# Forming more q-k blocks from stored q and k, and halving value products by an adding DMA

## The chip, the core and the metric

The kernel runs on one core of a Trainium2 chip. A core has a matmul engine (PE), a vector engine (DVE), a scalar engine (ACT), a general engine that here only issues DMAs (POOL), and SP, which issues DMAs too. Each engine works through its own queue in order and waits on semaphores for the others. Matmuls write to PSUM, eight banks of 128 x 512 fp32; everything else lies in SBUF, 128 partitions wide. The metric is device microseconds of one execution.

## The reference

One input `x` (2048 tokens, 1024 wide) goes through two branches that a sigmoid gate mixes. Branch A is dilated local attention with 32 heads of 32: each position looks at itself and at seven earlier positions in steps of two. Branch B is a gated GELU network with 3584 hidden columns.

```python
g = _sigmoid((x * gate_w).sum(-1, keepdims=True))
a = _A_ref(x, wqkv, wo)      # H = 32, Dh = 32, W = 8, dil = 2
b = _B_ref(x, w_gate, w_up, w_down)
return g * a + (1 - g) * b

# in _A_ref
idx = pos[:, None] - off[None, :]            # off = arange(8) * 2
logits = einsum("bhsd,bhswd->bhsw", q, kg) * scale
logits = where(mask, logits, -1e9)
o = einsum("bhsw,bhswd->bhsd", softmax(logits), vg)
return o.reshape(B, S, D) @ wo
# in _B_ref
h = gelu(x @ w_gate) * (x @ w_up)
return h @ w_down
```

## The kernel before, in words

All large products are done by Strassen's scheme (seven products for eight). The work before the last part is a row of 78 units. A unit forms two output tiles of 128 x 1024 from seven half-depth products, each of four matmuls of 128 x 512 (L366), 28 matmuls in all; ACT copies or evaluates the PSUM results (L374, L384, L389, L396, L372) and one DVE addition (L403) closes the unit. It reads the banks that the unit's last products wrote, and the unit's L22 product (in `p4`) writes one of these banks again, 12 matmuls after the last product that L403 waits for.

Units 0 and 1 belong to branch B (gate and up). Units 2 to 17 make q and k: two halves of the sequence (s = 0, 1), eight tiles (t) of 128 dimensions each. Units 18 to 25 make v, and the others up to 77 gate and up. Then `run_last` joins attention and hidden values in the down projection, again by Strassen's scheme, in two levels (L1046, L1079 and the DVE forms L1004 and L1012).

Between the units' L403s DVE does the attention. The planner is `run_bg`: after each unit it takes steps of background tasks in order of priority until a credit of about 4.7 us, by the costs that the tasks yield, is used up. `due` forces a task to end at a given unit. What the planner takes in a unit stands in DVE's queue between that unit's L403 and the next, so the order is fixed when the program is built.

The sequence is cut into eight blocks of 256 positions (`AC`), four for each half.

- q-k products, `qk_prods` and `qk_mult` (L598). For three of the four blocks of a half, each unit's q and k tile gives a product tile of 128 x 2048 (eight window positions by 256). `reduce_mm` (L603) sums the 32 dimensions of each head on PE, by matmuls with a block pattern that write 32 rows each, four beside each other, and accumulates over the eight tiles t in PSUM. For each pair of units 24 such matmuls stand in one slot of PE's queue.
- The fourth block of each half is formed later. `store_qk` writes its q and k columns to DRAM, `spill_load` brings them back, and `spill` multiplies them and adds four tiles together (L649) before the reduction, so that its two accumulated tiles need only 8 matmuls.
- `softmax` and `softmax_back` (L687 to L709) make the weights and store them (`w_d`, by POOL). They run in five groups: two blocks, one block, three blocks, one, one.
- Value products, `pv_all`. `pv_load` (SP) brings weights and values of a block. For each of eight tiles one product of 2048 elements (L745), and for each two tiles three foldings that halve 8 window positions to 4, 2 and 1 (L752). Products of the next tiles stand between the foldings, so that an operation seldom needs the one just before it. Results are stored to `o_d` by POOL.
- `t_forms` (L874) makes sums of the down weights and stores them to `t_d`; `sums_pair` (L323) makes sums of the gate and up weights; `h_store` (L254) multiplies gate and up.
- `gate_chunk` (L282, in two slots) forms the sigmoid's argument in bank 1, just after the reductions of that slot.

A slot is a place in a unit after its fifth product, where reductions queued in `slotq` and the gate's matmuls go:

```python
cur.p5()
extra = 0.0
if slotq:
    slotq.pop(0)()
    extra += 1.6 if b <= QE + 3 else 0.8
...
cur.p26()
...
run_bg(b, (4.7 if b < NQKV else 4.8) + extra)
```

Of the kernel before, what the change touches and what calls it, by code (L numbers as in the profile page):

```python
# [32 lines left out]
R_Q = 32  # L33
# [3 lines left out]
R_EX = (194.5, 81, 50, 81, 84)  # L37
# [15 lines left out]
R_O = (36, 32)  # L53
R_VB = (40, 48.25)
R_AB = (44.25, 52.5)
R_PROD2 = 56.5
# [12 lines left out]
def kernel(  # L69
# [51 lines left out]
    q_d = [tc.dram_tile([P, NT, AC], BF16, name=f"q_d{s}") for s in range(2)]  # L121
    k_d = [tc.dram_tile([P, NT, KV], BF16, name=f"k_d{s}") for s in range(2)]
# [9 lines left out]
    w_d = tc.dram_tile([NBLK, 32, NJ, SC], BF16, name="w_d")  # L132
# [4 lines left out]
    with tc.manual_schedule(engines={mybir.EngineType.PE, mybir.EngineType.DVE, mybir.EngineType.Activation,  # L137
# [357 lines left out]
        def h_task(G, U, i, s):  # L495
            h_store(G, U, i, s)
            yield 1.14 if i < NE_ else 2.35
# [28 lines left out]
        def store_qk(T, t, s):  # L526
            if s == 0:
                nc.scalar.copy(out=ktail[:, t, :], in_=T[:, 1, SUP - HALO:SUP])
            nc.gpsimd.dma_start(out=q_d[s][:, t, :], in_=T[:, 0, SUP - AC:SUP])
            nc.gpsimd.dma_start(out=k_d[s][:, t, :], in_=T[:, 1, SUP - KV:SUP])  # L530
# [42 lines left out]

        qb = [reg3(R_Q + 9 * i, NT, AC) for i in range(2)]
        kb = [reg3(R_Q + 9 * i + 4, NT, KV) for i in range(2)]
        vb = [reg3(R_VB[i], NT, KV) for i in range(2)]
        pr_off = [R_PR + 4 * i for i in range(4)] + [R_PROD + 4 * i for i in range(2)]
        prod = [reg3(o, NWIN, AC) for o in pr_off]
        attn_all = reg3(R_ATTN, NBLK, SC)
        mask = reg3(R_MASK, NWIN, SJ)  # L580
        ab_ = [reg4(R_AB[i], NJ, NWIN, SJ) for i in range(2)]
        ob_ = [reg3(R_O[i], NT, AC) for i in range(2)]
        prod2 = [reg4(R_PROD2 + 8 * i, 2, NJ, NWIN * SJ) for i in range(2)]
# [6 lines left out]
        pr_n = [0]  # L590

        def prod_tile():
            k = pr_n[0] % 6
            pr_n[0] += 1
            return prod[k]

        def qk_mult(dst, q, k):
            TT(out=dst, in0=q.rearrange("p (o s) -> p o s", o=1).to_broadcast([P, NWIN, AC]),  # L598
               in1=_win_ap(k, [[-DIL, NWIN], [1, AC]]), op=ALU.mult)

# [5 lines left out]
        ND = BPS - 1  # L606
        LGB = 5
        reduced, front, prods = [0], set(), {}

        def qk_prods(u, s, t):  # L610
            while reduced[0] < NT * s + t - t % 2:
                yield None
            out_ = []
            for a in range(ND):
                pr = prod_tile()
                qk_mult(pr, u.T[:, 0, a * AC:(a + 1) * AC], u.T[:, 1, a * AC:(a + 1) * AC])
                out_.append(pr)
                yield 1.14
            prods[t] = out_
            if t % 2:  # L620
                slotq.append(lambda: (qk_reduce(s, t - 1, prods[t - 1]), qk_reduce(s, t, out_)))

        def qk_reduce(s, t, out_):
            assert s == 0 or t > 0 or front == {0, 2}
            for a, pr in enumerate(out_):
                reduce_mm(bank(LGB + a), pr, t == 0, t == NT - 1)
            reduced[0] += 1
            if t == NT - 1:
                if s == 0:
                    bg(softmax(0, 2, LGB, 0), 1, now[0])  # L630
                    bg(softmax(2, 1, LGB + 2, 1), 1, now[0])
                else:
                    bg(softmax(BPS, 3, LGB, 2), 1, now[0])

        def spill_load(s):
            nc.sync.dma_start(out=qb[s], in_=q_d[s][:])
            nc.sync.dma_start(out=kb[s], in_=k_d[s][:])

        def spill(s):
            while reduced[0] < 2 * NT:  # L640
                yield None
            accs = []
            temps = [prod_tile() for _ in range(2)]

            def mult(t, dst):
                qk_mult(dst, qb[s][:, t, :], kb[s][:, t, HALO:HALO + AC])

            def add(g, t):
                TT(out=accs[g], in0=accs[g], in1=temps[t % 2], op=ALU.add)  # L649

            for g in range(NT // QG):
                accs.append(prod_tile())
                mult(QG * g, accs[g])
                yield 1.14
                for t in range(1, QG):
                    mult(QG * g + t, temps[t % 2])
                    yield 1.14
                    if t > 1:
                        add(g, t - 1)
                        yield 1.14  # L660
                add(g, QG - 1)
                yield 1.2
            slotq.append(lambda: spill_reduce(s, accs))
# [3 lines left out]
        def spill_reduce(s, accs):  # L667
            for g, acc in enumerate(accs):
                reduce_mm(bank(LGB + s), acc, g == 0, g == len(accs) - 1)
            bg(softmax(s * BPS + BPS - 1, 1, LGB + s, 3 + s), 1, now[0])  # L670
# [4 lines left out]
        def softmax(a, cnt, b0, e):  # L675
# [9 lines left out]
            m = md[:, (0, 2, 0, 3, 0)[e]:(0, 2, 0, 3, 0)[e] + cnt, :]  # L685
            assert e < 2 or ready >= {2: {0, 1, 2}, 3: {0, 1, 2}, 4: {4, 5, 6}}[e]
# [13 lines left out]
        def softmax_back(a, cnt, ee, e4, sw, m, bc):  # L700
            while a // BPS not in gated:
                yield None
            d = m
            V.tensor_reduce(out=d, in_=sw, axis=AX.X, op=ALU.add)
            yield 0.9 * cnt + 0.05
            V.reciprocal(out=d, in_=d)
            TT(out=d, in0=d, in1=gblk[:, a:a + cnt, :], op=ALU.mult)
            yield 0.65 * cnt
            TT(out=attn_all[:, a:a + cnt, :].rearrange("p a (w s) -> p a w s", w=NWIN), in0=e4, in1=bc(d), op=ALU.mult)  # L709
            yield 0.55 * cnt + 0.05  # L710
            for j in range(NJ):
# [3 lines left out]
            if a == 2 * BPS - 1:  # L715
                two[0] = True

        def pv_load(a, i):
            src = w_d[a].rearrange("h j n -> h (j n)")
            nc.sync.dma_start(out=ab_[i % 2].rearrange("p j w s -> p (j w s)"),  # L720
# [4 lines left out]
        PVO = (0, 1, 2, 4, 5, 6, 3, 7)  # L725

        def pv_all():
            for k in (0, 1):
                while PVO[k] not in ready:
                    yield None  # L730
            pv_load(PVO[0], 0)
            yield None
            for i, a in enumerate(PVO):
# [4 lines left out]
                if i == 0:  # L738
                    pv_task[0].prio = 5
                    tasks.sort(key=lambda t_: t_.prio)  # L740
                    yield None
                v, ab, o_ = vb[i % 2], ab_[i % 2], ob_[i % 2]

                def mult(t):
                    TT(out=prod2[(t // 2) % 2][:, t % 2], in0=ab,  # L745
                       in1=_win_ap(v[:, t, HALO:HALO + AC], [[SJ, NJ], [-DIL, NWIN], [1, SJ]]), op=ALU.mult)

                def fold(t, w):
                    pr = prod2[(t // 2) % 2]
                    h = lambda k: pr[:, :, :, k * w * SJ:(k + 1) * w * SJ]  # L750
                    out_ = h(0) if w > 1 else o_[:, t:t + 2, :].rearrange("p t (j s) -> p t j s", j=NJ)
                    TT(out=out_, in0=h(0), in1=h(1), op=ALU.add)  # L752

                mult(0)
                yield 1.14
                mult(1)
                yield 1.14
                for t in range(0, NT, 2):
                    if i + 1 == NBLK and t == 2:
                        load_A(Bs(0)["A12"], 0, 1, 0, 0, KX, False)  # L760
                    nxt = t + 2 < NT
                    if nxt:
                        mult(t + 2)
                        yield 1.14
                    fold(t, 4)
                    yield 1.14
                    if nxt:
                        mult(t + 3)
                        yield 1.14
                    fold(t, 2)  # L770
                    yield 0.68
                    fold(t, 1)
                    yield 0.4
                a0 = a % BPS % 2 * AC
                nc.gpsimd.dma_start(out=o_d[a // BPS][a % BPS // 2][:, :, a0:a0 + AC], in_=o_)
# [31 lines left out]
        bg(spill(0), 4, QE + 2)  # L807
        bg(spill(1), 4, QE + 2)
# [39 lines left out]
        N1 = 5  # L848
# [15 lines left out]
        def t_forms():  # L864
            for q in range(NQ):
                tf_q[0] = q
                if q in (N1 + 1, N1 + 2):
                    tft.prio = 3.9 if q == N1 + 1 else 4.5
# [17 lines left out]
        def tf_close():  # L886
            while tf_q[0] < N1:
                tft.step()
            tft.prio = 4.5
# [3 lines left out]
        at_end(TFE - 1, tf_close)  # L893
# [355 lines left out]
        for b in range(n):  # L1249
# [10 lines left out]
            if slotq:  # L1260
                slotq.pop(0)()
                extra += 1.6 if b <= QE + 3 else 0.8
# [45 lines left out]
```

## Time and profile before

| | before |
|---|---|
| median of 3 runs | 720.93 us (719.81 to 720.95) |
| profiled execution | 720.06 us, span 718.3 us |
| PE, DVE busy | 707.2 us, 673.2 us |
| ACT, POOL busy | 328.7 us, 134.5 us |
| granted TensorE clock | 1.00 |
| DMA | 162.04 MB, mean 226 GB/s |

Busy time is the union of an engine's instructions as the profiler recorded them. A group's row gives the source line, engine, operation, what it writes and reads with shapes, the count, the busy time and the mean of one, and then the idle time just before its instructions with what ended it. A timeline row gives start, length and engine of one instruction or of several alike in a row. A DMA row gives the size of one issue and the median time from issue to landing.

### The profile page before, as it was taken

To read this page: it belongs to the slowest core of one execution; us is meant where nothing else is said; L and a number is where in the kernel's file an instruction comes from. 1 tells how busy PE (TensorE), PEld (TensorE's weight loads), DVE (VectorE), ACT (ScalarE), POOL (GpSimd) and SP (SyncE) were. 2 spreads that over 40 slices of the span, in tenths; PEclk is the share of its full clock that TensorE was granted. 3 is DMA by queue.
4 is the path that set the end of the run, shared out by engine and by line. 5 is a ranking of instruction groups with operands and counts; after the bars stand their busy time and mean duration, and the time that the engine had idled before them with its cause. 6 is when DMAs were issued, how large, how long until landed. Compare 5 with 4: busy or idle time off the path is not lost. (4 is left out here: it accounts for less than half of the span.)

```text
span 718.3 us, 10752 instructions
## 1 busy us (share of the span) xinstructions
PE 707.2 (98%) x4051; PEld 408.2 (57%) x4107; DVE 673.2 (94%) x722; ACT 328.7 (46%) x600; POOL 134.5 (19%) x233
## 2 busy tenths in 40 slices
PE   8999999999999999999999999999999999999998
PEld 4466656655544444444444444444447886758887
DVE  2789989999999999999999999999999999899997
ACT  4554546444456665555555555555322321131431
POOL 1323544133210332121300000000210002110011
PEclk9999999999999999999999999999999999999999
DMA  9976643378264758574934836371891899995951
GB/s 276 284 183 219 229 142 122 106 247 304 102 205 127 231 197 252 175 221 149 294 115 152 280 123 214 124 288 59 300 427 52 307 401 396 420 429 223 379 213 60
DMA packets 92276, 162.04 MB, mean 226 GB/s; under 512 B 19280, under 2 KB 68848, under 8 KB 87872
## 3 DMA queue, kind: packets, MB, share of 16 engines
q1 hardware_dynamic: 75520, 105.46, 42.7%
q0 software_dynamic: 15984, 48.29, 19.3%
q10 hardware_dynamic: 720, 7.60, 2.7%
q8 instruction: 32, 0.52, 0.3%
q14 instruction: 20, 0.16, 0.1%
HBM read 112.17 MB, written 54.14 MB: 232 GB/s over the span
## 5 line engine op out<-in xcount | busy, mean ns | idle before, releaser
L366 PE MATMUL banks<-arena 128*128 128x512 bf16 x2136 | 472.1, 379 | 4.2 <-DVE arena L403 0.7
L366 PEld LDWEIGHTS <-arena 128*128 128x128 bf16 x2184 | 240.5, 111 | 235.3 <-issue 7.0
L1046 PE MATMUL banks<-arena 128*128 128x256 bf16 x1260 | 138.9, 273 | 0.8 <-DVE arena L1012 0.6
L1046 PEld LDWEIGHTS <-arena 128*128 128x128 bf16 x1260 | 123.1, 98 | 16.7 <-issue 1.5
L389 ACT COPY arena<-banks 128x512 f32<-128x512 f32 x78 | 45.8, 587 | 130.7 <-PE banks L366 130.7
L403 DVE TENSOR_TENSOR arena<-banks,arena 128x1024 bf16<-128x1024 f32 x78 | 95.2, 1221 | 11.0 <-PE banks L366 5.5
L374 ACT CAST arena<-banks 128x512 bf16<-128x512 f32 x102 | 59.7, 586 | 42.4 <-PE banks L366 42.4
L745 DVE TENSOR_TENSOR arena<-arena 128x2048 bf16<-128x2048 bf16 x64 | 77.0, 1220 | 0.5
L752 DVE TENSOR_TENSOR arena<-arena 128x2048 bf16<-128x2048 bf16 (+2 forms) x96 | 73.9, 776 | 1.0
L598 DVE TENSOR_TENSOR arena<-arena 128x2048 bf16<-128x2048 bf16 x64 | 74.7, 1219 | 0.1
L260 POOL DMA_DIRECT2D h_d<-arena x28 | 20.4, 730 | 226.5 <-DVE arena L254 195.4
L1079 PE MATMUL banks<-arena 128*128 128x512 bf16 x282 | 62.5, 379 | 0.3
L396 ACT COPY banks<-banks 128x512 f32<-128x512 f32 x78 | 44.5, 570 | 21.8 <-PE banks L366 20.0
L1004 DVE TENSOR_TENSOR arena<-arena 128x2304 bf16<-128x2304 bf16 x40 | 53.3, 1352 | 0.5
L384 ACT COPY banks<-banks 128x512 f32<-128x512 f32 x78 | 45.0, 576 | 13.6 <-PE banks L366 12.1
L1051 ACT COPY banks<-banks 128x256 f32<-128x256 f32 x60 | 21.4, 356 | 60.9 <-PE banks L1046 60.7
L1079 PEld LDWEIGHTS <-arena 128*128 128x128 bf16 x288 | 28.2, 98 | 33.5
L927 DVE TENSOR_TENSOR arena<-arena 128x2048 bf16<-128x2048 bf16 (+1 forms) x40 | 41.8, 1111 | 1.3 <-DMA arena<-h_d 1.3
L372 ACT ACTIVATE arena<-banks 128x512 bf16<-128x512 f32 x54 | 32.2, 597 | 15.4 <-PE banks L366 15.3
L323 DVE TENSOR_TENSOR arena<-arena 128x1024 bf16<-128x1024 bf16 x60 | 38.6, 685 | 0.5
L1012 DVE TENSOR_TENSOR arena<-arena 128x2304 bf16<-128x2304 bf16 x28 | 37.7, 1351 | 0.2
L254 DVE TENSOR_TENSOR arena<-arena 128x2048 bf16<-128x2048 bf16 x28 | 34.0, 1216 | 1.9 <-ACT arena L251 1.4
(93 smaller groups left out, 435.8 us busy)
## 6 DMA issues: line engine op xcount, KB each, us to landing
arena<-t_d SPq DMA_DIRECT2D x8, 2304.0 KB, 14.4
h_d<-arena POOLq DMA_DIRECT2D x28, 512.0 KB, 4.3
arena<-w_c SPq DMA_DIRECT2D x12, 1152.0 KB, 14.1
t_d<-arena POOLq DMA_DIRECT2D x36, 256.0 KB, 4.3
arena<-h_d SPq DMA_DIRECT2D x6, 1536.0 KB, 12.7
arena<-in_B_w_gate_dram SPq DMA_DIRECT2D x15, 512.0 KB, 5.7
arena<-in_B_w_up_dram SPq DMA_DIRECT2D x15, 512.0 KB, 5.3
arena<-in_B_w_down_dram SPq DMA_DIRECT2D x28, 256.0 KB, 6.6
```

The costliest lines, as they stand in the source:

```text
L366: self.pe = nc.tensor.matmul(ps, lhsT=self.L[form](kt), rhs=rhs[:, kt, :], start=(start and kt == 0), stop=(kt == HK - 1), skip_group_chec ...
L374: nc.scalar.copy(out=o_, in_=i_)
L384: nc.scalar.copy(out=self.Y, in_=self.X)
L389: nc.scalar.copy(out=self.p5s, in_=self.V)
L396: nc.scalar.copy(out=self.Z, in_=self.Y)
L403: TT(out=self.T[:, :, c2s], in0=pair, in1=self.p5s.rearrange("p (o n) -> p o n", o=1).to_broadcast([P, 2, SC]), op=ALU.add)
L598: TT(out=dst, in0=q.rearrange("p (o s) -> p o s", o=1).to_broadcast([P, NWIN, AC]), in1=_win_ap(k, [[-DIL, NWIN], [1, AC]]), op=ALU.mult)
L745: TT(out=prod2[(t // 2) % 2][:, t % 2], in0=ab, in1=_win_ap(v[:, t, HALO:HALO + AC], [[SJ, NJ], [-DIL, NWIN], [1, SJ]]), op=ALU.mult)
L752: TT(out=out_, in0=h(0), in1=h(1), op=ALU.add)
L1004: TT(out=o_, in0=a, in1=b_, op=op)
L1046: nc.tensor.matmul(c(i, h, j), lhsT=l[:, kt, j * P:(j + 1) * P], rhs=r[:, kt, :], start=False, stop=(kt == KH - 1), skip_group_check=True)
L1079: nc.tensor.matmul(ps, lhsT=L[:, i, j * P:(j + 1) * P], rhs=R[:, i, :], start=(start and q == 0), stop=(q == NK - 1), skip_group_check=not ...
```

## The change

Four blocks, not two, are now formed later from stored q and k: the last two of each half. `q_d` and `k_d` hold twice the columns. `qk_prods` handles the first two blocks of a half in each unit; for each pair of units the two units' products are added on DVE (`two_adds`) before one reduction of 8 matmuls. `spill` is one task that goes through blocks 2, 6, 3, 7; each group of four tiles is added in a tree (two tiles to two, then one to one). Where the planner has credit for it, two products or two additions are one DVE operation of 4096 elements (`qk_mult2`, `pair_at`). Softmax runs in six groups: two of two blocks and four of one.

The value products start when all q-k blocks are done, in three product tiles (four from when the last weights are ready) rather than two. A product of two tiles is one operation where credit allows. The first halving is a DMA from POOL that adds the upper half of the tile to the lower half (`accum_op=ALU.add`), if another product tile is free; the smaller foldings of that tile come at least two units later (`LAG`). If none is free, DVE does all three. Of 32 first halvings, 20 go to the DMA in the built program. The weights are stored in another order (`w_d`: window, then position), in runs of 64 elements. T forms join two of their four subtractions in one operation, and six of nine groups are made early, not five.

```diff
-    q_d = [tc.dram_tile([P, NT, AC], BF16, name=f"q_d{s}") for s in range(2)]
-    k_d = [tc.dram_tile([P, NT, KV], BF16, name=f"k_d{s}") for s in range(2)]
+    q_d = [tc.dram_tile([P, NT, 2 * AC], BF16, name=f"q_d{s}") for s in range(2)]
+    k_d = [tc.dram_tile([P, NT, AC + KV], BF16, name=f"k_d{s}") for s in range(2)]
...
+        def pair_at(a, b):
+            return _win_ap(reg(a, NWIN * AC), [[int((b - a) * KB), 2], [1, NWIN * AC]])
+
+        def qk_mult2(dst, q, k, sq, sk):
+            TT(out=dst, in0=_win_ap(q, [[sq, 2], [0, NWIN], [1, AC]]),
+               in1=_win_ap(k, [[sk, 2], [-DIL, NWIN], [1, AC]]), op=ALU.mult)
...
+        def two_mults(x, q, k, sq, sk):
+            if credit[0] > 1.5:
+                qk_mult2(pair_at(*x), q, k, sq, sk)
+                yield 2.21
+            else:
+                for j in range(2):
+                    qk_mult(reg3(x[j], NWIN, AC), _win_ap(q[:, j * sq:j * sq + 1], [[1, AC]]),
+                            _win_ap(k[:, j * sk:j * sk + 1], [[1, AC]]))
+                    yield 1.14
...
         def qk_prods(u, s, t):
-            while reduced[0] < NT * s + t - t % 2:
+            pair = (NT * s + t) // 2
+            while len(reduced) < pair - 1:
                 yield None
-            out_ = []
-            for a in range(ND):
-                pr = prod_tile()
-                qk_mult(pr, u.T[:, 0, a * AC:(a + 1) * AC], u.T[:, 1, a * AC:(a + 1) * AC])
-                out_.append(pr)
-                yield 1.14
-            prods[t] = out_
+            acc, tmp = tuple(pr_off[2 * (pair % 2):2 * (pair % 2) + 2]), tuple(pr_off[4:6])
+            yield from two_mults(tmp if t % 2 else acc, u.T[:, 0, 0:2 * AC], u.T[:, 1, 0:2 * AC], AC, AC)
             if t % 2:
-                slotq.append(lambda: (qk_reduce(s, t - 1, prods[t - 1]), qk_reduce(s, t, out_)))
+                yield from two_adds(acc, tmp)
+                slotq.append(lambda: qk_reduce(s, pair, acc))
...
+        SPILL = (2, 6, 3, 7)
+        def spill_load(j):
+            s, c = divmod(SPILL[j], BPS)
+            c = (c - 2) * AC
+            nc.sync.dma_start(out=qb[j % 2], in_=q_d[s][:, :, c:c + AC])
+            nc.sync.dma_start(out=kb[j % 2], in_=k_d[s][:, :, c:c + KV])
...
+                    for i, ef in enumerate((x, y)):
+                        t = QG * g + 2 * i
+                        yield from two_mults(ef, flat(q)[:, t * AC:(t + 2) * AC], flat(k)[:, t * KV + HALO:(t + 2) * KV], AC, KV)
+                    yield from two_adds(x, y)
+                    TT(out=tile_at(x[0]), in0=tile_at(x[0]), in1=tile_at(x[1]), op=ALU.add)
                     yield 1.14
...
             for j in range(NJ):
-                nc.gpsimd.dma_start(out=w_d[a:a + cnt, :, j, :].rearrange("a h n -> h a n"),
-                                    in_=attn_all[32 * j:32 * j + 32, a:a + cnt, :])
+                for i in range(a, a + cnt):
+                    nc.gpsimd.dma_start(out=w_d[i][:, :, j * SJ:(j + 1) * SJ],
+                                        in_=attn_all[32 * j:32 * j + 32, i, :].rearrange("h (w s) -> h w s", w=NWIN))
...
-        PVO = (0, 1, 2, 4, 5, 6, 3, 7)
+        PVO = (0, 1, BPS, BPS + 1) + SPILL
+        LAG = 2
...
+                    while behind and now[0] >= behind[0][0] + LAG:
+                        yield from folds(*behind.pop(0)[1:], 2, 1)
...
+                    k = free.pop(0)
+                    if credit[0] > 1.5:
+                        mult(k, i, t, 0, 2)
+                        yield 2.21
+                    else:
+                        for m0 in range(2):
+                            mult(k, i, t, m0, 1)
+                            yield 1.14
+                    if free and (i, t) < (NBLK - 1, NT - 4):
+                        lo, hi = half(k, 4)
+                        nc.gpsimd.dma_start(out=lo, in_=hi, accum_op=ALU.add)
+                        behind.append((now[0], k, i, a, t))
+                    else:
+                        yield from folds(k, i, a, t, 4, 2, 1)
...
-        N1 = 5
+        N1 = 6
...
-                for o_, a, b_ in ((r11, r12, r11), (r12, r22, r12), (r22, r22, r11), (r21, r21, r22)):
+                n_ = NP * SC
+                both = _win_ap(flat(r11), [[n_, 2], [1, n_]])
+                TT(out=both, in0=_win_ap(flat(r12), [[2 * n_, 2], [1, n_]]), in1=both, op=ALU.subtract)
+                yield 1.14
+                for o_, a, b_ in ((r22, r22, r11), (r21, r21, r22)):
                     TT(out=flat(o_), in0=flat(a), in1=flat(b_), op=ALU.subtract)
-                    yield 0.71
+                    yield 0.61
...
             if slotq:
                 slotq.pop(0)()
-                extra += 1.6 if b <= QE + 3 else 0.8
+                extra += 0.6
```

More of the change, by code (lines that the diff above doesn't have):

```diff
@@ L52 @@
 R_S = (16, 24)
[L53 to L56, printed above, removed]
+R_O = (44.25, 32)
+R_QB = (32, 47.75)
+R_VB = (36, 48.25)
+R_AB = (40.25, 52.5)
+R_PROD2 = (56.5, 64.5, 83, 72.5)
 R_BUF = tuple(1 + 18 * k for k in range(10))
@@ L610, in qk_prods, with two_adds @@
+        def two_adds(x, y):
+            if credit[0] > 1.5:
+                TT(out=pair_at(*x), in0=pair_at(*x), in1=pair_at(*y), op=ALU.add)
+                yield 2.21
+            else:
+                for j in range(2):
+                    TT(out=tile_at(x[j]), in0=tile_at(x[j]), in1=tile_at(y[j]), op=ALU.add)
+                    yield 1.14
         def qk_prods(u, s, t):
-            while reduced[0] < NT * s + t - t % 2:
+            pair = (NT * s + t) // 2
+            while len(reduced) < pair - 1:
@@ new lines, in qk_reduce @@
+        def qk_reduce(s, pair, acc):
+            p = pair % (NT // 2)
+            assert pair == len(reduced) and (s == 0 or p > 0 or front == {0})
+            for a, o in enumerate(acc):
+                reduce_mm(bank(LGB + a), reg3(o, NWIN, AC), p == 0, p == NT // 2 - 1)
+            reduced.append(pair)
+            if p == NT // 2 - 1:
+                bg(softmax(BPS * s, 2, LGB, s, 0), 1, now[0])
+        SPILL = (2, 6, 3, 7)
[4 more added lines that the diff above has]
+            nc.sync.dma_start(out=kb[j % 2], in_=k_d[s][:, :, c:c + KV])
@@ L672, with spill_reduce, softmax @@
+        slotq = []
+        def spill_reduce(j, a, accs):
+            b_ = LGB + (2, 0, 1, 2)[j]
+            assert BPS in front and (j < 3 or SPILL[0] in front)
+            for g, o in enumerate(accs):
+                reduce_mm(bank(b_), reg3(o, NWIN, AC), g == 0, g == len(accs) - 1)
+            spilled.append(j)
+            bg(softmax(a, 1, b_, 2 + j % 2, 2 + j % 2), 1, now[0])
         ready = set()
         md = consts.tile([P, 4, SJ], F32, name="md")
-        def softmax(a, cnt, b0, e):
+        def softmax(a, cnt, b0, e, d0):
@@ L723, in pv_load, with mult, half, folds @@
             nc.sync.dma_start(out=vb[i % 2], in_=v_d[:, :, a * AC:a * AC + KV])
-        PVO = (0, 1, 2, 4, 5, 6, 3, 7)
+        PVO = (0, 1, BPS, BPS + 1) + SPILL
+        LAG = 2
         def pv_all():
-            for k in (0, 1):
-                while PVO[k] not in ready:
-                    yield None
+            while not (at_spill[0] >= len(SPILL) - 1 and ready >= set(PVO[:-1])):
+                yield None
             pv_load(PVO[0], 0)
             yield None
+            while at_spill[0] < len(SPILL) or len(spilled) < len(SPILL):
+                yield None
+            pv_task[0].prio = 5
+            tasks.sort(key=lambda t_: t_.prio)
+            free, behind, left = list(range(len(prod2) - 1)), [], {i: NT // 2 for i in range(NBLK)}
+            def mult(k, i, t, m0, m):
+                TT(out=prod2[k][:, m0:m0 + m, :],
+                   in0=flat(ab_[i % 2]).rearrange("p (o n) -> p o n", o=1).to_broadcast([P, m, NWIN * AC]),
+                   in1=_win_ap(vb[i % 2][:, t + m0, HALO:HALO + AC], [[KV, m], [-DIL, NWIN], [1, AC]]), op=ALU.mult)
+            def half(k, w):
+                return [prod2[k][:, :, c * w * AC:(c + 1) * w * AC] for c in range(2)]
+            def folds(k, i, a, t, *w):
+                o_ = ob_[i % 2]
+                for w_ in w:
+                    lo, hi = half(k, w_)
+                    TT(out=lo if w_ > 1 else o_[:, t:t + 2, :], in0=lo, in1=hi, op=ALU.add)
+                    yield 0.08 + 0.267 * w_
+                assert k < 2 or not pd
+                free.append(k)
+                left[i] -= 1
+                if left[i] == 0:
+                    a0 = a % BPS % 2 * AC
+                    nc.gpsimd.dma_start(out=o_d[a // BPS][a % BPS // 2][:, :, a0:a0 + AC], in_=o_)
+            late, a12 = [], []
             for i, a in enumerate(PVO):
@@ L754, in pv_all @@
[L754 to L773, printed above, removed]
@@ L774, in pv_all @@
-                a0 = a % BPS % 2 * AC
-                nc.gpsimd.dma_start(out=o_d[a // BPS][a % BPS // 2][:, :, a0:a0 + AC], in_=o_)
+                if PVO[-1] in ready and i > 0 and not late:
+                    late.append(True)
+                    free.append(len(prod2) - 1)
+                for t in range(0, NT, 2):
+                    if i + 1 == NBLK and t >= 4 and left[i - 1] == 0 and not a12:
+                        a12.append(True)
+                        load_A(Bs(0)["A12"], 0, 1, 0, 0, KX, False)
+                    while behind and now[0] >= behind[0][0] + LAG:
+                        yield from folds(*behind.pop(0)[1:], 2, 1)
+                    if now[0] >= n - 13:
+                        free[:] = [k for k in free if k < 2]
+                        assert free
+                    k = free.pop(0)
+                    if credit[0] > 1.5:
+                        mult(k, i, t, 0, 2)
+                        yield 2.21
+                    else:
[6 more added lines that the diff above has]
+                        behind.append((now[0], k, i, a, t))
+                    else:
+                        yield from folds(k, i, a, t, 4, 2, 1)
@@ L776, in pv_all @@
+            assert a12
+            while behind:
+                while now[0] < behind[0][0] + LAG:
+                    yield None
+                yield from folds(*behind.pop(0)[1:], 2, 1)
             while now[0] < n - 6:
```

123 lines of the change are left out of this document (44 added, 79 removed).

## The prediction

> **What bounds the kernel now.** I read the page's first part, then busy time by stage, then the timelines of PE and DVE, then the groups by shape, last the DMA issues.
>
> ```profile
> PE 707.2 (98%) x4051; PEld 408.2 (57%) x4107; DVE 673.2 (94%) x722; ACT 328.7 (46%) x600; POOL 134.5 (19%) x233
> ```
>
> Two engines are nearly full, so a saving on one is worth what the other lets through. The 78 units each end in one L403 on DVE; I cut the span at the L403 of unit 0 (31.4), of unit 42 (301.9) and of unit 77 (513.0).
>
> ```profile
> core 0: us, PE busy (x) PEld busy (x) DVE busy (x) ACT busy (x) POOL busy (x), PEclk, DMA share, GB/s
> 31.40:301.90 270.50, 267.72 (x1375) 146.94 (x1401) 257.80 (x278) 144.88 (x258) 82.29 (x147) 1.00 0.59 191
> 301.90:513.00 211.10, 209.82 (x959) 95.52 (x977) 205.70 (x224) 116.91 (x192) 27.47 (x37) 1.00 0.56 183
> 513.00:718.30 205.30, 200.93 (x1545) 151.47 (x1550) 194.50 (x199) 52.52 (x125) 18.11 (x33) 1.00 0.76 304
> ```
>
> Stage I (q-k work) leaves DVE 12.7 us of idle, stage II (value work) only 5.4. PE sets the pace in both: L403 of unit 42 starts at 301.93, that of unit 75 at 501.33, which is 6.04 us a unit, 28 matmuls of 0.216. DMA is half busy, so bandwidth does not bind in stages I and II.
>
> ```profile
> 103.80 1.03 PE L366 MATMUL banks<-arena 128*128 128x512 bf16 x4
> 104.76 1.48 PE L603 MATMUL banks<-arena,ones_r 128*32 128x512 bf16 x24
> 106.17 6.05 PE L366 MATMUL banks<-arena 128*128 128x512 bf16 x26
> ...
> 206.75 3.83 PE L366 MATMUL banks<-arena 128*128 128x512 bf16 x17
> 210.52 0.61 PE L603 MATMUL banks<-arena,ones_r 128*32 128x512 bf16 x8
> 211.06 3.19 PE L366 MATMUL banks<-arena 128*128 128x512 bf16 x14
> ```
>
> This prices a block of reducing matmuls by what it adds between unit matmuls. The last L366 before the 24 starts at 103.80+3x0.216 = 104.45, the next after it at 106.17: 1.72, less the 0.216 it would be anyway, 1.51 us. For 8 the same reading gives 0.64. So a block has 0.2 us of its own, and dividing 13.1 us of busy time by 208 matmuls would overstate what is saved.
>
> ```profile
> 175.60 1.22 DVE L598 TENSOR_TENSOR arena<-arena 128x2048 bf16<-128x2048 bf16 x1
> 176.73 1.22 DVE L649 TENSOR_TENSOR arena<-arena 128x2048 bf16<-128x2048 bf16 x1
> 177.99 1.23 DVE L598 TENSOR_TENSOR arena<-arena 128x2048 bf16<-128x2048 bf16 x1
> ```
>
> DVE operations follow each other 0.08 us before the row's duration is over (175.60 to 176.73), but 0.035 after it where the second needs the one just before (176.73 to 177.99).
>
> ```profile
> L403 DVE TENSOR_TENSOR arena<-banks,arena 128x1024 bf16<-128x1024 f32 x78 | 95.2, 1221 | 11.0 <-PE banks L366 5.5 <-issue 3.5 <-ACT arena L411 0.9
> L745 DVE TENSOR_TENSOR arena<-arena 128x2048 bf16<-128x2048 bf16 x64 | 77.0, 1220 | 0.5
> L752 DVE TENSOR_TENSOR arena<-arena 128x2048 bf16<-128x2048 bf16 x32 | 39.0, 1218 | 0.0
> L752 DVE TENSOR_TENSOR arena<-arena 128x1024 bf16<-128x1024 bf16 x32 | 21.9, 685 | 0.2
> L752 DVE TENSOR_TENSOR arena<-arena 128x512 bf16<-128x512 bf16 x32 | 13.5, 423 | 0.9
> L649 DVE TENSOR_TENSOR arena<-arena 128x2048 bf16<-128x2048 bf16 x12 | 14.6, 1218 | 0.0
> ```
>
> 512, 1024 and 2048 elements at 423, 685 and 1218 ns are a line: 0.151 us and 0.522 ns an element. A 4096-wide one is not in the trace; on the line it takes 2.29, 2.20 as a step in a row, which saves 0.07 over two of 2048. The bounds are 2.07 (no fixed cost) and 2.44 (two whole ones); I take the line.
>
> **PE's side.** Before: 8 blocks of 24 and 2 of 8, 8x1.51+2x0.64 = 13.3 us. After, because products are added ahead of the reduction: 12 blocks of 8, 7.7 us. **-5.6 us**, all of it in stage I and on the path.
>
> **DVE's side.** Counting the built order of the changed kernel with the steps above (the same count for before gives 257.6 and 205.7 for the two stages, against 257.8 and 205.7 in the windows):
> - q-k products: 64 tiles, now 24 wide and 16 single: 73.1 to 71.4.
> - tile additions: 12 become 40 (13 wide, 14 single): 13.8 to 46.6.
> - value products: 64, now 19 wide and 26 single: 74.4 to 71.7.
> - foldings: 32 first halvings become 12, the 64 smaller ones stay: 70.0 to 49.0. Only 20 of 32 go to the adding DMA.
> - T forms (two 1024-wide subtractions made one): 23.6 to 22.5. Softmax in six groups, not five: +1.0.
>
> Sum: +7.3 us; 255.4 in stage I (-2.2), 215.2 in stage II (+9.5). The second exceeds the 211.1 that the stage lasts now: value work starts at unit 42, not 33, and still has to end by unit 76.
>
> **What becomes late.** PE lets L403 lag 1.3 us: after a unit's last product it has 12 matmuls (2.6 us) until it writes the bank that L403 (1.22) reads. Lag beyond that stops PE. I kept a balance over the units: DVE work less PE time, never below zero.
> - Unit 13 of the changed order holds four T-form subtractions, a wide product and a softmax back end, 9.7 us against 6.04. Lag 3.7, so PE waits 1.9 to 2.4 us; unit 15 has 7.05 and a reduction in the next slot waits for its additions, 1.3 more. Together +3.2. Five smaller waits up to unit 41: +0.5.
> - The gate's matmuls (L282) stand in two slots behind a 24-block; they write bank 1, which ACT copies (L389, 0.59) after starting some 0.28 late. With no block in one slot and 8 in the other: +0.9 and +0.2.
> - Against this go PE's waits of stage I in before. 42 units at 6.04 are 253.7, with 13.3 and 1.2 for the gate 268.2 of 270.5: 2.3 us, of which 0.6 at 43 us (weight sums) stays. -1.7.
> - Stage II: 215.2 less 211.1 is +4.1, of which PE tolerates 1.3 at the end, and 0.9 is the idle that L403 of unit 77 now has before it. +1.9.
>
> Sum: -5.6+3.2+0.5+1.1-1.7+1.9 = **-0.6 us**. The profiled execution took 720.06 (718.3 and 1.8 around it), 0.9 under the median of three; on the median's scale 720.93-0.6 = 720.3.
>
> **Costed at nothing, with their cover.** Doubled q and k stores (548 and 545 ns an issue on POOL, same count), 32 weight stores instead of 20 at 0.53 each, in runs of 64 elements: POOL is at 30% in stage I; behind them on POOL stand the q-k stores, whose tiles are four deep. Four loads of q and k from SP in 512-byte runs: the nearest row, 544-byte runs of v_d, lands in 8.3 us at worst; the first pair issues at 138 now and is needed past 164. Later ones and the value loads stand in SP's queue before weight loads, which are wanted three units (18 us) on. Each cover gone would cost its lateness in full.
>
> **The adding DMA** is the term with no row. 20 times 512 KB from the tile into itself, issued by POOL after the product; the fold waits for it, and behind it in DVE's queue stands L403 and so PE. Summing the steps between, the shortest cover is 8.8 us, three are 10.2 to 10.3, three 11.2 to 11.7, the rest up to 17.
>
> ```profile
> h_d<-arena POOLq DMA_DIRECT2D x28, 512.0 KB, 4.3
> ...
> w_c<-in_B_w_down_dram POOLq DMA_DIRECT2D x12, 384.0 KB, 6.3
> o_d<-arena POOLq DMA_DIRECT2D x8, 512.0 KB, 7.1
> ```
>
> Lowest row: h_d at its quickest, 3.3; highest: o_d doubled, since the destination is read too, 14.2. I take 7, nearest to h_d by size and run, with more traffic: no stall. [...]
>
> **Rivals.**
> 1. DVE absorbs the bunches, as lag and not as PE waits, and the -5.6 mostly stays: unit 13's +3.2 falls to 1, stage II's 1.9 to 1. About 717.2. For it: POOL and ACT have room, and DVE's idle falls by 7 us whichever way. Against: L403 holds a bank that PE must write.
> 2. The adding DMA lands late, slower. It decides from 9 us on. At 11 us the four shortest covers miss by 2.2, 0.8, 0.8 and 0.7: 4.4 us, in a stage with no idle left, so 724.7; at 12, seven miss by 9.9: 730. For it: w_c copies and h_d stores stand in the same queue, and loads on half-busy DMA engines ran up to 21 us at the end of before. Against: all POOL rows of stage II have medians of 7.1 or less.
> 3. It does less than it says, as fewer products run double: the built order excludes it for the counts; a wide operation at 2.44 instead of 2.29 would add 56x0.15 = 8 us to DVE, some 5 to the time: 725.
>
> **How the numbers follow.** 0.2% is 1.4 us, about what measurement tells from no change. The forecast, 718.5 to 722 around 720.3, gets 0.43; 0.11 of it lies below 719.5 and 0.02 above 722.4. Rival 1 gets 0.27, rival 2 with 3 gets 0.30. So faster 0.38, same 0.30, slower 0.32. The range leaves out half a tenth of the quick side (716.5) and the worst of rival 2 (726).
>
> **What would show it.** Twelve 8-blocks at L602, each 0.64; DVE near 255 and 215 us in stages I and II; a PE gap of 2 to 4 us around unit 14; L403 of unit 42 some 2.5 us earlier than 301.9, and PE entering the last part less than 1 us earlier. Foldings (L777) that wait for a DMA mean rival 2; a first unit of stage II over 5 us earlier, rival 1. Wrong altogether if wide operations miss the line, or if a load of q, k or v is waited for.

## The result, and the profile after

The changed kernel takes 756.37 us (median of 4 runs, 754.87 to 761.38) against 720.73 for the kernel before (4 runs): ratio 1.0509, interval 1.0457 to 1.0561. The forecast was 720.3, so 36 us above it are to be explained. The profiled execution took 754.87 us with a span of 753.0.

The same three stretches as before, cut at the L403 of units 0, 42 and 77 (columns: stretch; its length, then busy time of PE, weight loads, DVE, ACT, POOL; granted clock, DMA share, GB/s):

```profile
31.63:305.07 273.44, 265.80 (x1282) 143.75 (x1281) 254.97 (x227) 147.09 (x260) 86.77 (x154) 0.99 0.61 190
305.07:546.88 241.81, 220.43 (x1000) 98.03 (x999) 213.98 (x221) 120.13 (x195) 55.91 (x63) 0.96 0.79 216
546.88:753.00 206.12, 198.43 (x1537) 149.91 (x1535) 194.54 (x200) 52.53 (x125) 18.07 (x33) 1.00 0.77 308
```

Stage I is 2.9 us longer than before (270.5), stage II 30.7 (211.1), the rest 0.8. DVE is busy for 214.0 us of stage II, yet the stage lasts 241.8: the time is idle time, not work. The waits of DVE, then of PE, in the changed kernel (engine, tile and line, what ended the wait; total us, times, longest):

```profile
DVE arena L323 <- DMA arena<-in_B_w_up_dram: 21.9, 3, 10.8
...
PE banks L366 <- DVE arena L403: 28.9, 12, 10.5
```

L323 forms the sums of the gate and up weights of a pair of units. Three times, in units 51, 59 and 63 (10.78, 4.49 and 6.64 us), its weights are not there; before, no such wait is among DVE's. DVE's order is fixed, so L403 of the next unit stands behind L323, and PE behind L403. The first of them on DVE, whose L403 of unit 51 was over at 363.3:

```profile
374.11 2.62 DVE L323 TENSOR_TENSOR arena<-arena 128x1024 bf16<-128x1024 bf16 x4 [10.78 <-DMA arena<-in_B_w_up_dram]
```

and the SP queue that issues those weights (start, time on the queue, line, transfer):

```profile
351.06 0.53 SPq L746 DMA_DIRECT2D arena<-w_d  x1
351.70 1.46 SPq L749 DMA_DIRECT2D arena<-v_d  x1
353.20 2.35 SPq L167 DMA_DIRECT2D arena<-in_B_w_gate_dram  x1
355.60 5.91 SPq L167 DMA_DIRECT2D arena<-in_B_w_up_dram  x1
```

The weights are issued when the value load (`pv_load`, w_d and v_d) ahead of them on SP is through, and that waits until DVE has made the last product from the tiles that it overwrites (L766 is over at 351.04, w_d goes out at 351.06). Counted from the L403 of unit 42 (305.07), the gate load goes out after 48.1 us and the up load after 50.5. In the run with later value loads (below), where nothing stands ahead of them, it is 40.3 and 46.3; these are the times at which they are due, so here they are 7.8 and 4.2 us late. In the kernel before value loads stand ahead of the same weights too,

```profile
341.70 0.54 SPq L720 DMA_DIRECT2D arena<-w_d  x1
342.28 0.95 SPq L723 DMA_DIRECT2D arena<-v_d  x1
343.33 0.95 SPq L167 DMA_DIRECT2D arena<-in_B_w_gate_dram  x1
347.60 1.03 SPq L167 DMA_DIRECT2D arena<-in_B_w_up_dram  x1
```

but the weights go out 41.4 and 45.7 us after its L403 of unit 42 (301.93), close to these due times. In the changed kernel they also travel slowly. DMA of the changed kernel from 350 to 374 us (queues with packets, MB and share of 16 engines; then issues with KB each and us to landing),

```profile
q0 software_dynamic: 1584, 4.46, 68.7%
q1 hardware_dynamic: 3271, 2.13, 29.0%
...
arena<-in_B_w_gate_dram SPq DMA_DIRECT2D x1, 512.0 KB, 18.0
arena<-in_B_w_up_dram SPq DMA_DIRECT2D x1, 512.0 KB, 18.4
```

and of the kernel before from 341 to 356 us, with the same transfers on SP:

```profile
q0 software_dynamic: 637, 2.35, 49.5%
q1 hardware_dynamic: 3264, 2.13, 45.6%
...
arena<-in_B_w_gate_dram SPq DMA_DIRECT2D x1, 512.0 KB, 8.6
...
arena<-in_B_w_up_dram SPq DMA_DIRECT2D x1, 512.0 KB, 8.1
```

SP's queue (q1) moves the same 2.13 MB in both, in 24 us here and in 15 before. POOL's queue (q0), where the adding DMAs run beside stores and copies of weights, moves nearly twice the bytes meanwhile, and the weights take 18 us instead of 8 to 9 (12 to 14 for those of units 59 and 63). From the up load's due issue (351.4) to the end of L403 (363.3) there are 11.9 us, which is its cover; 4.2 late and 18.4 on the way leave 10.7 too little, the wait of unit 51.

The longest wait cost more than itself: after 10.54 us of idle PE starts at half rate (busy time of the engines, granted clock after the weight-load to POOL columns, in the two stretches that follow):

```profile
380.10:385.60 5.50, 5.48 (x14) 1.93 (x14) 4.43 (x3) 2.68 (x4) 3.23 (x3) 0.51 0.50 134
385.60:391.00 5.40, 5.40 (x27) 2.45 (x26) 4.45 (x5) 2.58 (x5) 0.00 (x0) 1.00 1.06 193
```

14 matmuls in the first 5.5 us, 27 in the next 5.4: start to start 0.427 us, then 0.216. The length of the idle does not tell how many matmuls are slow: 2.55 us before 129.2 us were followed by nine slow ones, 5.99 before 465.8 by twelve, 3.72 before 435.0 by none. What decides it is not shown.

### The profile page after: what moved, and what is told of

Its sections match the earlier page's. It is cut to its first block, busy times and chain, and to the rows that moved or that the text cites. A ratio compares the mean times of both kernels' runs of the same rounds, so it can differ in the third digit from the quotient of the medians.

```text
span 753.0 us, 10608 instructions
## 1 busy us (share of the span) xinstructions
PE 714.1 (95%) x3995; PEld 406.7 (54%) x3995; DVE 678.7 (90%) x671; ACT 334.3 (44%) x605; POOL 167.6 (22%) x265
## 5 line engine op out<-in xcount | busy, mean ns | idle before, releaser
L366 PE MATMUL banks<-arena 128*128 128x512 bf16 x2184 | 483.4, 383 | 29.3 <-DVE arena L403 28.9
L1096 PEld LDWEIGHTS <-arena 128*128 128x128 bf16 x1260 | 123.0, 98 | 18.4 <-DVE arena L1062 2.1
L403 DVE TENSOR_TENSOR arena<-banks,arena 128x1024 bf16<-128x1024 f32 x78 | 95.0, 1218 | 11.8 <-PE banks L366 6.7
L374 ACT CAST arena<-banks 128x512 bf16<-128x512 f32 x102 | 59.7, 585 | 40.8 <-PE banks L366 40.5
L766 DVE TENSOR_TENSOR arena<-arena 128x2048 bf16<-128x2048 bf16 (+1 forms) x45 | 74.1, 1667 | 0.1
L1129 PE MATMUL banks<-arena 128*128 128x512 bf16 x288 | 63.0, 379 | 0.5 <-DMA arena<-h_d 0.5
L323 DVE TENSOR_TENSOR arena<-arena 128x1024 bf16<-128x1024 bf16 x60 | 38.7, 686 | 22.5 <-DMA arena<-in_B_w_up_dram 21.9
L597 DVE TENSOR_TENSOR arena<-arena 128x4096 bf16<-128x4096 bf16 x24 | 54.7, 2283 | 2.0 <-ACT arena L722 1.5
L777 DVE TENSOR_TENSOR arena<-arena 128x512 bf16<-128x512 bf16 (+2 forms) x76 | 49.3, 660 | 2.6 <-DMA arena<-arena 1.0
L977 DVE TENSOR_TENSOR arena<-arena 128x2048 bf16<-128x2048 bf16 (+1 forms) x40 | 41.8, 1109 | 3.2 <-DMA arena<-h_d 3.2
L372 ACT ACTIVATE arena<-banks 128x512 bf16<-128x512 f32 x54 | 32.2, 597 | 17.0 <-PE banks L366 16.6
L254 DVE TENSOR_TENSOR arena<-arena 128x2048 bf16<-128x2048 bf16 x28 | 34.0, 1214 | 1.4 <-ACT arena L251 1.4
```

The lines of the kernel that those rows point to most:

```text
L366: self.pe = nc.tensor.matmul(ps, lhsT=self.L[form](kt), rhs=rhs[:, kt, :], start=(start and kt == 0), stop=(kt == HK - 1), skip_group_chec ...
L374: nc.scalar.copy(out=o_, in_=i_)
L403: TT(out=self.T[:, :, c2s], in0=pair, in1=self.p5s.rearrange("p (o n) -> p o n", o=1).to_broadcast([P, 2, SC]), op=ALU.add)
L597: TT(out=dst, in0=_win_ap(q, [[sq, 2], [0, NWIN], [1, AC]]), in1=_win_ap(k, [[sk, 2], [-DIL, NWIN], [1, AC]]), op=ALU.mult)
L766: TT(out=prod2[k][:, m0:m0 + m, :], in0=flat(ab_[i % 2]).rearrange("p (o n) -> p o n", o=1).to_broadcast([P, m, NWIN * AC]), in1=_win_ap(v ...
L777: TT(out=lo if w_ > 1 else o_[:, t:t + 2, :], in0=lo, in1=hi, op=ALU.add)
```

## The experiments

Two theories for stage II. **Order**: the weights are late because they stand behind the value load in SP's queue. **Contention**: they are late because the adding DMAs fill the DMA engines. Of the first five kernels four change one thing each, and one makes the first two changes at once.

**Value loads later.**

```
-  (head of block i)      pv_load(PVO[i + 1], i + 1)
+  (at t == 4)            pv_load(PVO[i + 1], i + 1)
```

> The changed kernel, with the loads of the next block's values issued in the middle of a block of value products instead of at its head, so that on SP they no longer stand waiting ahead of the weight loads of the next pair. Theory A (order on SP): the gate-weight loads of units 51, 59 and 63 are issued 6 to 8 us earlier, DVE's wait of L323 for weights falls from 21.9 us to under 8, PE's wait of L366 for L403 from 28.9 us to under 12, and the time is 732 to 740 us. Theory B (the weights travel too slowly beside the adding DMAs and the copies of w_c): L323 still waits 15 us or more, and the time is 750 us or more.

736.06 us, ratio 1.0211 (1.0173 to 1.025). L323's waits fell from 21.9 to 3.2 us; SP's queue for unit 51:

```profile
350.00 0.37 SPq L167 DMA_DIRECT2D arena<-in_B_w_gate_dram  x1
356.04 0.37 SPq L167 DMA_DIRECT2D arena<-in_B_w_up_dram  x1
356.51 5.84 SPq L746 DMA_DIRECT2D arena<-w_d  x1
```

The order theory's numbers hold but for one: PE's wait for L403 is 14.6 us, not under 12, and some 11 of it lie in stage I. These two loads still took 16.6 and 13.3 us (wait 1.76), those of unit 59, issued at 401.1 and 407.1 ahead of their value load, 5.1 and 6.8.

**No adding DMA.**

```
-  nc.gpsimd.dma_start(out=lo, in_=hi, accum_op=ALU.add)
```

> The changed kernel with the 20 adding DMAs left out and nothing in their place: 20 of the first halvings of value products are not done, all else stays where it is. Theory B (contention): the weight loads of units 51, 59 and 63 land in 7 to 9 us instead of 12 to 18, the wait of L323 falls from 21.9 us to under 6, and the time is 725 to 732 us. Theory A (order): the loads are still issued 6 to 8 us late, 12 us or more of the wait of L323 stays, and the time is 742 us or more.

731.75 us, ratio 1.0152 (1.0132 to 1.0172). No L323 waits in stage II, though the weights of unit 51 are issued as late as ever, at 353.5 (47.2 us into the stage, 6.9 late). Their landings:

```profile
arena<-in_B_w_gate_dram SPq DMA_DIRECT2D x1, 512.0 KB, 7.4
arena<-in_B_w_up_dram SPq DMA_DIRECT2D x1, 512.0 KB, 8.2
```

So the contention theory's numbers hold too. Each theory alone predicted that the other's removal would leave most of the wait; both were wrong in that.

**Both at once.**

> Both single removals at once: value loads in the middle of a block, and the 20 adding DMAs left out with nothing in their place (20 first halvings are not done). The first saved 20 us alone and the second 24 us. Theory (the two together make one wait, and either one's absence leaves it covered): the second adds nothing, 728 to 734 us, no wait of L323 for weights over 1 us. Rival (two separate costs that add up): about 711 us.

733.99 us, ratio 1.0176 (1.0142 to 1.0209): nothing is added. No L323 of stage II waits; one of stage I (unit 26) waits 1.6. The length of stage II in the four kernels:

| | adding DMAs | without |
|---|---|---|
| value load at head of block | 241.8 | 215.3 |
| value load in its middle | 217.9 | 215.4 |

The two make one wait: here a load may be late, or slow, but not both. (Stage I is the same program in these four and took 273.4 to 278.8 us, with waits for loads that differ, so the total times are blurred by some 5 us.)

**Copies earlier.**

```
-  at(NQKV + 10 + 6 * m_ + e_, ...)
+  at(NQKV - 6 + 6 * m_ + e_, ...)
```

> The changed kernel with the three sets of copies of gate and up weights in DRAM (L883, due in units 36 to 54) due 16 units earlier, so that most lie in stage I. If the copies are what the weight loads share the queues with, the load of unit 51 lands in about 10 us instead of 18, its wait of 10.8 us falls below 4, and the time is 740 to 747 us; those of units 59 and 63 stay. If the copies do not matter, the waits of L323 stay within 3 us of 21.9 and the time is 753 to 758 us.

754.91 us, ratio 1.0475 (1.0427 to 1.0522). (The copies are of the down and output weights, not of gate and up as the expectation has it.) Unit 51's wait fell from 10.78 to 4.64, those of units 59 and 63 stayed at 4.49 and 7.24. Stage II is 6.7 us shorter and stage I 6.5 longer; at 279.9 that is hardly above what it takes with the copies unmoved (up to 278.8). Neither expectation holds whole: the copies make 6 of the 10.8 us at unit 51 and nothing at the other two.

**Five early tiles.**

```
-  N1 = 6
+  N1 = 5
```

> The changed kernel with N1 = 5 instead of 6, so that the tile buffers that must be free by TFE do not force the work of two sums into unit 13. Theory of stage I: the 9.7 us unit 13 and PE's 2.9 us stall with the slow restart behind it are gone, and L403 of unit 42 starts 3 to 5 us earlier than in the changed kernel (300 to 302 us instead of 305.1); the waits of L323 in the second stage stay near 22 us and the time is 750 to 753 us. Rival: the work of unit 13 only moves to other units of the stage, and L403 of unit 42 starts within 1 us of 305.1.

766.21 us, ratio 1.0634 (1.0595 to 1.0672). Unit 13 went from 9.70 to 7.11 us and PE's stall behind it is gone, but L403 of unit 42 started at 303.78, between the two theories, and in stage II unit 63 waits 9.05 us for weights instead of 6.64, and unit 67 5.3 besides (29.9 us in all). Inconclusive for stage I.

**Halvings on DVE.**

```
-  nc.gpsimd.dma_start(out=lo, in_=hi, accum_op=ALU.add)
+  TT(out=lo, in0=lo, in1=hi, op=ALU.add)
```

> The changed kernel with each of the 20 adding DMAs replaced by the same addition on DVE, at the same place. By what the run without the adding DMAs showed, the weight loads land in 7 to 8 us and no L323 waits for them. If DVE is then the bound of the second stage, the 20 additions cost their step of 1.14 us in full, 23 us on top of the 731.8 us of that run: 752 to 757 us, so that the adding DMAs gain about what they cost. Rival: the stage has room for half of them, 738 to 745 us.

757.14 us, ratio 1.0499 (1.0477 to 1.0522), 0.1 above the expected range: stage II is 239.9, which is the 215.3 without these additions and 20 of 1.22. The adding DMAs take 24.5 us off stage II (215.3 against 239.9) and give 26.5 back (241.8), nearly all through the weights.

**The value part alone**, on the kernel before: `pv_all` and the weights' layout of the changed kernel, the q-k side, T forms and softmax groups of before.

> The kernel before, with the value part of the change alone: four product tiles, wide multiplications, first halvings by adding DMA, the weights in the new layout; q-k blocks, reductions and T forms stay as before. Counted in the built order, DVE has 26 us less to do up to unit 77 than before. Theory (order and contention together): the weight loads still stand behind the value loads in SP's queue, so L323 waits for weights by 4 us or more in all, and with DVE's room part of it is caught up: 721 to 730 us. Rival (only DVE's load made the waits hurt): no L323 waits over 1 us, PE sets the pace, and the time is 715 to 721 us.

773.63 us, ratio 1.0731 (1.0708 to 1.0753): worse than the whole change, and worse than either expectation. DVE is only 84% busy. DVE's waits, and landings from 280 to 480 us:

```profile
DVE arena L323 <- DMA arena<-in_B_w_up_dram: 42.9, 6, 9.5
```

```profile
arena<-in_B_w_up_dram SPq DMA_DIRECT2D x7, 512.0 KB, 16.9
...
arena<-in_B_w_gate_dram SPq DMA_DIRECT2D x6, 512.0 KB, 15.3
arena<-v_d SPq DMA_DIRECT2D x5, 544.0 KB, 13.9
```

In the kernel before these medians are 5.0, 5.4 and 5.7. Value work starts in unit 33 here, not 42, so six pairs of weights meet it, not three. Room on DVE catches nothing up: in units 65 to 74 DVE idles 1.4 to 4.8 us per unit ahead of L403 while PE goes on at 6.03 to 6.06.

**The value part alone, value loads later.**

> The value part alone, on the kernel before, with the value loads issued in the middle of a block. That part alone took 773.6 us with 42.9 us of L323's waits for weights. Theory: the weights then go ahead of the value loads on SP and land in 5 to 7 us instead of 15 to 17; L323 waits under 4 us in all, PE sets the pace of the second stage again, and the time is 717 to 724 us, level with the kernel before, since the 26 us taken off DVE are on an engine that PE already holds back. Rival (the adding DMAs slow the weights whatever the order): 735 us or more.

732.99 us, ratio 1.0165 (1.0131 to 1.02): 40 us less by the order alone, but above the 717 to 724 expected, and below the rival's 735. The weights now land in 6.9 and 7.4 us (medians) and L323 waits 2.1. What is left in stage II (222.3 us) is that wait, a fold's wait of 2.78 in unit 60 for its adding DMA, DVE's wait of 2.79 in unit 75 for ACT, and slow restarts of PE behind them (mean granted clock 0.993). So even with 26 us less on DVE the value part gains nothing: in units 65 to 74 PE sets the pace here too, at 6.03 to 6.06 us a unit.

**Order and halo.** Stage I: POOL's queue in the changed kernel,

```profile
98.53 0.54 POOL L529 DMA_DIRECT2D q_d<-arena  x1 [0.61 <-DVE arena L403]
101.28 0.54 POOL L530 DMA_DIRECT2D k_d<-arena  x1 [2.21 <-ACT arena L523]
101.81 0.77 POOL L298 DMA_DIRECT2D zc<-z_d  x1
```

where in the kernel before the k store follows the q store at once (99.77 and 100.30). The wider store begins with 16 columns (the halo, which the block's first positions look back at) that lie in the half of the tile that `p4` evicts last, by ACT (L374, at 100.40; the row names L523, the small copy that follows it on ACT). The gate's load of zc stands behind the store, and DVE waits 2.4 us for zc (L300, unit 11). Late issue is not all of it: zc took 5.1 us to land, against 2.3 in the kernel before; why is not shown.

```
-  nc.gpsimd.dma_start(out=k_d[s][:, t, :], in_=T[:, 1, SUP - AC - KV:SUP])
+  for f in late_k[:]: late_k.remove(f); f()
+  nc.gpsimd.dma_start(out=k_d[s][:, t, HALO:], in_=T[:, 1, SUP - 2 * AC:SUP])
+  late_k.append(lambda: nc.gpsimd.dma_start(out=k_d[s][:, t, 0:HALO], in_=T[:, 1, SUP - AC - KV:SUP - 2 * AC]))
```

> The changed kernel with the value loads issued in the middle of a block (as in the first run) and the k store of a tile cut in two: its 16 columns that ACT evicts last are stored when the next tile is, so that POOL's queue does not wait for ACT. Theory of stage I: L300's wait for zc falls from 2.7 to below 0.5 us, PE's late restart goes with it, and the time is 2 to 6 us below that run's 736.1: 730 to 734 us. Rival: those waits are covered and only the name changes, 735 to 737 us.

727.75 us, ratio 1.0104 (1.0074 to 1.0134), 8.3 below the run with the order alone and 2 below the range expected. The wait for zc is gone (zc lands in 2.5); PE's stall behind unit 13 is 1.8 us instead of 2.6. Stage I is 271.3, stage II 216.4. Since the unrepaired stage I took 273.4 to 278.8, the store is worth between 2 and 7 us.

**Order, halo, five early tiles.**

> The run with both repairs (value loads later, k store cut in two), and N1 = 5 besides, so that no two T-form sets are forced into unit 13. Theory: unit 13 is 7.1 us instead of 9.7, PE's stall near 126 us is gone, L403 of unit 42 starts at 298 to 303 us, and the time is 724 to 730 us. Rival: N1 = 5 moves the lump to the second stage, where DVE is full, and the weights of unit 67 come late again as in the run with N1 = 5 alone: 733 to 740 us.

725.33 us, ratio 1.0059 (1.0038 to 1.0081): L403 of unit 42 at 300.62, as the theory has it. The extra work of unit 13 was worth 2 us once the rest was out of the way.

**The same with the copies earlier, and the same with later q and k loads.**

> The best version so far (value loads later, k store cut in two, N1 = 5; 725.3 us) with the copies of down weights in DRAM due 16 units earlier, out of the stretch where the adding DMAs run. Theory: the waits of units 50, 51 and 62 (0.7, 1.5 and 0.3 us) go, and the time is 722 to 724.5 us. Rival: the copies then slow the loads of stage I by as much, 725 to 729 us.

725.7 us, ratio 1.0065 (1.0044 to 1.0085): units 51 and 62 lose their waits (0 and 0.2 left), unit 26 has 3.07 instead of 1.46, the rival's case; the time is the same.

```
-  spill_load(j + 2)
+  at(now[0] + 1, lambda j=j: spill_load(j + 2))
```

> The best version so far (725.3 us) with the later loads of stored q and k issued behind the weight loads of the same unit instead of ahead of them. Theory: the wait of L323 in unit 26 (1.5 us) goes, the time is 723 to 724.5 us. Rival: the q-k products then wait for their loads instead, 725 us or more.

724.38 us, ratio 1.0054 (1.0036 to 1.0073): unit 26's wait is gone, and fold waits (1.42 and 0.75 in units 50 and 62) keep stage II at 216.5. The time lies in the range of the theory, but 0.95 us is less than the spread of its own runs (722.7 to 727.5). No version beat the kernel before.

## Why the prediction was wrong

**Work on the engines: right.** One of the changed kernel's groups (count, total us, mean ns, idle before), and one block of eight between unit matmuls:

```profile
L766 DVE TENSOR_TENSOR arena<-arena 128x4096 bf16<-128x4096 bf16 x19 | 43.4, 2283 | 0.0
```

```profile
124.16 0.62 PE L602 MATMUL banks<-arena,ones_r 128*32 128x512 bf16 x8
124.71 1.95 PE L366 MATMUL banks<-arena 128*128 128x512 bf16 x8
```

The wide operations lie on the line (2.28 against 2.29), the 96 reducing matmuls come in eights, and DVE's busy time is 255.0 and 214.0 against 255.4 and 215.2. With the waits taken out stage II lasts 215.3 to 215.4, the counted DVE work to 0.2 us.

**Stage II, +1.9: mis-sized by 2.** Without waits it is +4.2 to +4.3. That PE tolerates 1.3 at the end, and that 0.9 of idle would be used, gave nothing back; the rest of the span is no shorter (205.9 and 206.0 with both repairs, against 205.3).

**The adding DMA: right where it was looked at.**

```profile
arena<-arena POOLq DMA_DIRECT2D x20, 512.0 KB, 7.1
```

7 was taken, and folds waited 1.0 us in all; rival 2 didn't happen. What failed is what these DMAs do to others on the same engines: the weights of unit 51 took 18.0 and 18.4 us beside them, 7.4 and 8.2 in the run without them. "DMA is half busy, so bandwidth does not bind" was read from the mean of a stage (0.56), while the kernel before already shows 1.03 from 343.3 to 356; the changed one holds 0.98 from 350 to 374.

**"Costed at nothing": the step that failed.** The prediction named the value loads that stand ahead of the weight loads, 18 us of cover, and lateness beyond it as a cost in full. It then put the term at nothing without working it out. 18 us is the gate load's cover; the up load, issued last, has 11.9. And neither the value load's own wait (4.2 for the up load of unit 51) was taken off it, nor the landing let grow beside the new transfers (18.4, not 8). The three waits (21.9), the DVE work (+4.1), the fold's wait (1.0) and DVE's idle behind slow restarts of PE (1.9 and 0.7) make 29.6 of stage II's 30.7.

**Stage I, forecast -2.5, measured +2.9.** -5.6 for PE's reductions fits the best repaired kernel, 269.4 against 270.5 with 4.6 us of DVE's waits for loads and ACT left in units 15 to 33, though no run takes the reductions alone. The gap in PE's work around unit 14 came (2.6 us), and making that unit's work smaller gave back 1.8 (271.3 to 269.4), where 1.9 to 2.4 was taken. "POOL is at 30%" missed that the wider k store waits for another engine, which was the 2.4 us at unit 11. The run with that store cut in two has neither this wait nor the slow restart behind unit 13 (1.9), but its stage I is only 2.2 of the 5.4 us between forecast and result shorter (273.4 to 271.3), because other waits stand in it (2.8 in unit 2, 1.2 for k in unit 15, 1.0 for weights in unit 26). So the rest of stage I's difference is not shown. Of the smaller waits, L597's 1.5 for ACT's exponential (unit 33) is new and stood in no term.

**The rivals.** No term of the sum allowed for PE's half rate after a stall (2.6 us of DVE's idle in stage II, some 1.9 at 129 us). Rival 1 did not happen: DVE's bunches did reach PE, which waited 2.6 us behind unit 13. Nothing in the range was above 726, since all rivals that ended slower were DVE or fold waits; "a load of q, k or v is waited for" stood as what would make it wrong altogether, with no price. A load was waited for, though of weights.

## What to carry to other kernels

For every load, write down its cover, the time from its due issue to its use, and take off it both how long the instruction ahead of it on the queue may wait, and the landing beside the new transfers: a cover that holds against either alone may fail against both. Read the DMA share of the stretch in which the loads travel, not of a stage, and count work moved from a compute engine to DMA as traffic beside the other loads (here 18 us for the weights of unit 51 instead of 7.4 and 8.2). For a store that is made wider, ask which engine writes its columns last, and what stands behind it on its queue: here the k store waited 2.21 us for ACT, and the load of zc behind it.

## What was not expected of the hardware

In the stretch from 350 to 374 us a packet of POOL's queue holds an engine for 0.17 us on the mean (68.7% of 16 engines for 24 us, 1584 packets), one of SP's queue for 0.034 (29.0%, 3271 packets). The same sum for the kernel before, from 341 to 356 us, gives 0.19 and 0.034. So the packets are alike in both, and what grew is how much POOL's queue had to move beside the weights (2.35 MB in 15 us, 4.46 in 24). How the engines divide their time between the two queues is not shown, and no run here separates the landings of 18 us beside the adding DMAs and of 8 without them from plain lack of bandwidth.

The issue of an adding DMA takes 1.2 us on POOL (median of 20 rows in the changed kernel), that of a plain store of the same 512 KB (h_d) 0.75.
